# Attention scores in PSUM: three buffers of two banks, visits of up to four units, and VectorE's clamps in pairs

## The chip, the cores and the metric

The kernel runs on one core of a Trainium2 chip. The metric is device time in microseconds, from the first to the last instruction of the core. The kernel before takes 862.6 us (median of three runs, 862.32 to 862.9). An engine runs its own list of instructions in order, and waits on semaphores for the others. TensorE (PE) multiplies matrices and writes to PSUM; PSUM has eight banks of 512 fp32 columns on 128 partitions. ScalarE (ACT) computes the exponentials, VectorE (DVE) copies, clamps and multiplies, GpSimd (POOL) does small scalings, and SyncE (SP) issues transfers.

## The reference, cut to what matters

```python
x = A_x                                    # 1 x 2048 x 640, bf16
g = sigmoid((x * gate_w).sum(-1, keepdims=True))
# A: full attention, 32 heads of 20
scores = einsum("bhqd,bhkd->bhqk", q, k) * 20 ** -0.5
a = (softmax(scores) @ v) @ A_wo
# B: local attention over 8 positions, 2 apart: pos, pos-2, ..., pos-14
logits = where(mask, einsum("bhsd,bhswd->bhsw", q, k[pos - 2 * w]) * 20 ** -0.5, -1e9)
b = (softmax(logits) over w, times v[pos - 2 * w]) @ B_wo
return g * a + (1 - g) * b
```

Branch A is 32 heads x 2048 queries x 2048 keys of exponentials. The kernel calls a piece of 128 keys x 512 queries of one head a *unit*: 32 x 16 x 4 = 2048 units. Each one needs a QK matmul into one PSUM bank, an exponential into SBUF as bf16, and a matmul with V that accumulates in the bank `obank`.

## The kernel before

Most units take their exponential on ScalarE. Some take it on VectorE: the score, already scaled, is clamped and written as a 16-bit integer whose bits read as bf16 are a rough power of two, and three shifted copies with weights (the copies `eD`, and V scaled by GpSimd, `vS`) smooth the error. Four units of one key block and four heads share the same steps.

The whole order of instructions is made on the host by a small scheduler: each task has an assumed duration and an assumed latency to its readers, and side work (projections, branch B, the output projection) is put where TensorE and VectorE are thought to be free.

```python
LAT = {"pe": 0.18, "act": 0.06, "dve": 0.08, "pool": 0.1, "sp": 0.1}   # assumed latency to a reader, by writer
SWITCH = 0.11                                                           # change of TensorE's tiling mode
# ... (cut)
    score = [ps(1536, "score0"), ps(1536, "score1")]      # two buffers of three banks
    obank = ps(512, "obank")
    sbank = ps(512, "side0")
    BANKS = [(sbank, 0), (score[0], 1024), (score[1], 1024)]   # banks for side work; the third of a buffer may be lent
# ... (cut)
    ebuf = [sb([P, 1536], BF16, "ebuf%d" % i) for i in range(NE)]       # NE = 5
# ... (cut)
    def next_tile():
        s = len(tiles)
        x = 1 + s % 2
        # ...
        n = 3 if free else 2       # three units for ScalarE if the third bank is free,
        # ...                      # or two, and one for VectorE ("ride") in the third bank
    def qk(s):
        # ... two or three matmuls, each with 32 rows (one head), into the buffer s % 2
        t = T("pe", 0.215, fn, ..., mode="row")
        if rides[s]:
            run_dve(t.end + LAT["pe"] - RFILL)
            t = T("dve", 0.69, lambda e: e.tensor_scalar(
                uD[d % 2][:, 512 * i:512 * (i + 1)].bitcast(I16), side[x], UOFF, 0.0, op0=ALU.add, op1=ALU.max), ...)
    def exp(s):
        n = len(tiles[s])
        exps[s] = T("act", actc(512 * n), lambda e: e.activation(
            ebuf[s % NE][:, 0:512 * n], score[s % 2][:, 0:512 * n], ACTF.Exp, scale=LN2 / STEP), ...)
# ... (cut)
    def filler(limit):     # matmuls whose result nobody reads, where TensorE would be empty
        # ...
# ... the main loop, per visit s: choose units, QK, exp, attention times V for earlier visits, then side work:
            lim = (exps[s - 1].end if s >= 1 else sch.avail["act"]) + SLACK[max(0, len(us) - 2)]   # SLACK = (0.3, 0.68)
            spend(lim)
```

A *visit* is one such step: QK matmuls for the units of one turn, each unit in a bank of its own. The matmuls of a visit use separate row quarters of the array and run beside one another.

Of the kernel before, what the change touches and what calls it, by code (L numbers as in the profile page):

```python
# [14 lines left out]
P = 128  # L15
# [39 lines left out]
LAT = {"pe": 0.18, "act": 0.06, "dve": 0.08, "pool": 0.1, "sp": 0.1}  # L55
# [20 lines left out]
class _Sched:  # L76
# [49 lines left out]
    def task(self, stream, dur, fn, reads=(), writes=(), dma=False, accum=(), mode="full", nd=1, iss=0.75):  # L126
# [27 lines left out]
        for d in t.deps:  # L154
            d.mark = True
            start = max(start, d.end + LAT[d.stream])
# [104 lines left out]
def _build(ctx, nc, A_x, A_wqkv, A_wo, B_wqkv, B_wo, gate_w, out):  # L261
# [9 lines left out]
    score = [ps(1536, "score0"), ps(1536, "score1")]  # L271
    obank = ps(512, "obank")
    sbank = ps(512, "side0")
    BANKS = [(sbank, 0), (score[0], 1024), (score[1], 1024)]
    NB = len(BANKS)
    side = [t_[:, o_:o_ + 512] for t_, o_ in BANKS]
    sap = lambda b, off, dims: _ap(BANKS[b][0], BANKS[b][1] + off, dims)


    NE = 5  # L280
# [14 lines left out]
    ebuf = [sb([P, 1536], BF16, "ebuf%d" % i) for i in range(NE)]  # L295
# [32 lines left out]
    repB = [sb([P, 2 * TOK], BF16, "repB%d" % i) for i in range(2)]  # L328
# [133 lines left out]
    xheld = [None]  # L462
# [327 lines left out]
    def gen_b(u):  # L790
# [55 lines left out]


# [17 lines left out]
        def taps(w4):  # L865
            T("sp", 2.0 + 0.75 * 4, lambda e: [e.dma_start(repB[w4 % 2][32 * i:32 * i + 32, :], eB[32 * w4:32 * w4 + 32, :])
                                               for i in range(4)], reads=["eB"], writes=[("repB", w4 % 2)], dma=True, nd=4)

        taps(0)
        taps(1)  # L870
        for w4 in range(4):
            for hh in range(2):
                w = 4 * hh + w4
                yield ("dve", DVE_AHEAD, sch.ready(("repB", w4 % 2)))
                vs = vB[:, :, PADB - DIL * w:PADB - DIL * w + TOK]
                rr = _ap(repB[w4 % 2], hh * TOK, [[0, CN], [1, TOK]])
                TB(dvc(CN * TOK, 2), lambda e, w=w, vs=vs, rr=rr: e.tensor_tensor(prodB(w), vs, rr, ALU.mult),  # L877
                  reads=["vB", ("repB", w4 % 2)], writes=[("prod", w)])
            if w4 < 2:
                taps(w4 + 2)  # L880
# [72 lines left out]
    def tail():  # L953
# [14 lines left out]
        b3 = score[1]  # L968
        mm(("score", 1), [fold_mms(b3[:, blk * P:(blk + 1) * P], blk, q, 512, D, False)[0] for blk in range(4)], False)
# [3 lines left out]
        for blk in range(2):  # L973
            mm(("score", 0), fold_mms(score[0][:, blk * 512:(blk + 1) * 512], blk, q, 0, 512, False), False)
        T("dve", dvc(512), lambda e: e.tensor_tensor(
            _ap(stage, 3 * 1024 + 512, [[D, 4], [1, P]]), _ap(b3, 0, [[P, 4], [1, P]]),
            stage[:, 2048:3072].bitcast(FP32).rearrange("p (b c) -> p b c", c=P), ALU.add),
          reads=[("score", 1), ("pre", 2)], writes=["tout_r"])
# [4 lines left out]
        for blk in range(2):  # L983
            T("dve", dvc(512), lambda e, blk=blk: e.tensor_tensor(
                tcol(blk, 0, 512), score[0][:, blk * 512:(blk + 1) * 512], pre(blk), ALU.add),
              reads=[("score", 0), ("pre", blk)], writes=[("tout", blk)])
# [50 lines left out]
    DVE_AHEAD = 0.56  # L1037
    DAHEAD = 0.5

    def step(ent, limit, force):  # L1040
# [14 lines left out]
        elif req[0] == "bank":  # L1055
            best = None
            for b in range(NB):
                if not bank_used[b] and b != xheld[0] and (best is None or max(bank_free[b], now) < max(bank_free[best], now)):
                    best = b
            if best is None or sum(bank_used) == NB - 1 or (not force and bank_free[best] > now):  # L1060
# [15 lines left out]
    BOOST = 4.1  # L1076
    XBOOST = 4.0
    XPRIO = 2.5
    XLATE = 6.3
    XT0 = 144.0  # L1080
    XT1 = 860.0

    def xprio():
        return XPRIO if bdone[0] >= (sch.avail["pe"] - XT0) / (XT1 - XT0) * BALL else XLATE

# [31 lines left out]
    def turn(tcc, c0, c1, s_):  # L1117
        xt, xo = XOFF[tcc]

        def fn(e):  # L1120
            ins = None
            for c in range(c0, c1):
                for blk in range(4):
                    o = score[s_][:, (c - c0) * 512 + blk * P:(c - c0) * 512 + (blk + 1) * P]
# [5 lines left out]
          writes=[("score", s_)] + ([("side", 1)] if c1 - c0 == 3 else []))  # L1130
# [6 lines left out]
    def x_out(tcc):  # L1137
        cols = slice(tcc * 512, (tcc + 1) * 512)
        T("act", actc(1536), lambda e: e.activation(  # L1139
            xT[:, 0:3, cols], _ap(score[0], 0, [[512, 3], [1, 512]]), ACTF.Copy), reads=[("score", 0), ("side", 1)], writes=[("xT", tcc, 0)])  # L1140
# [527 lines left out]
```

## Time and profile before

| | |
|---|---|
| time, median of three | 862.6 us |
| span of the profiled run | 860.4 us |
| visits | 732 |
| exps of 1024 / 1536 columns | 458 / 273 (and one of 512) |
| units clamped by VectorE | 312, each 512 wide |
| first exp starts / last exp ends | 20.7 / 848.5 us |
| busy in 0 to 20 us: PE / DVE / ACT | 16.6 / 13.4 / 10.6 us |
| busy in 840 to 860.4 us: PE / DVE / ACT | 15.3 / 6.1 / 9.2 us |
| TensorE's granted clock | 0.998 |

The profile is of one execution. Its first part gives each engine's busy time, its share of the span and its instructions; its second part cuts the span into 40 slices with a digit for the tenths of busy time. A group of instructions is one row: line, engine, operation, output and input, how often; then its busy time and the mean length of one; then the time the engine was idle just before them and what ended it. "L1432 ACT ... ebuf<-score" are the exponentials, "L1409 PE ... score<-qT,kT" the QK matmuls, "L1422 DVE ... uD<-score" the clamps, "L728 DVE ... eD<-uD" the shifted copies, "L1477 PE ... obank" attention times V, "L1498 PE" the filler and "L489 PE" side work. "PEld" is the loading of weights, at which TensorE's waits show. The waits are rows of: who waited, for whom, microseconds in total, times, the longest. "issue" is time in which nothing was waited for that the profile shows. A timeline row has start, length, what, and in brackets the idle time ahead of it.

### The profile page before, as it was taken

Reading aid. Unit: us, or ns where it says so; the run is one execution under the profiler, and the core shown is the slowest. Engines: PE = TensorE matmul, PEld = TensorE weight load, DVE = VectorE, ACT = ScalarE, POOL = GpSimd, SP = SyncE. Lnnn points to the kernel's source line nnn. Section 1 sums busy time; section 2 is a strip of 40 time slices with the busy share of each in tenths; the row PEclk is TensorE's granted clock in tenths of the full one; section 3 lists DMA queues with packets and bytes.
Section 4 is the critical chain, followed back from the end, with each engine's and each line's share of the span. In section 5 each row is a group of like instructions: output and inputs, shape, how many; then the busy total and the mean of one; then the engine's idle time right before and its main releaser. Section 6 shows DMA issues by size and latency. Waiting matters only on the chain.

```text
span 860.4 us, 30961 instructions
## 1 busy us (share of the span) xinstructions
PE 837.2 (97%) x13299; PEld 310.4 (36%) x13302; DVE 692.4 (80%) x1178; ACT 820.2 (95%) x766; POOL 220.4 (26%) x333
## 2 busy tenths in 40 slices
PE   8999999999999999999999999999999999999997
PEld 4333333343333433333333333333333333333323
DVE  6567787898888889887988879789798878989763
ACT  5999999999999999999999999999999999999994
POOL 5032042721322222221111223222142223123310
PEclk9999999999999999999999999999999999999999
DMA  9112231001010100011010000110010001100000
GB/s 300 33 30 54 45 73 32 16 13 30 25 28 20 38 11 21 5 44 39 18 33 17 6 19 21 32 47 8 20 28 20 6 17 33 46 6 21 14 6 32
DMA packets 40892, 28.16 MB, mean 33 GB/s; under 512 B 23733, under 2 KB 39557, under 8 KB 40757
## 3 DMA queue, kind: packets, MB, share of 16 engines
q1 hardware_dynamic: 40756, 26.20, 11.7%
q8 instruction: 105, 1.72, 0.8%
q14 instruction: 31, 0.25, 0.1%
HBM read 11.94 MB, written 2.62 MB: 17 GB/s over the span
## 4 chain that ended last, share of the span: by engine, by line
PE 77%; ACT 15%; DVE 4%; issue 3%; POOL 1%; DMA 1%; DVEq 0%; ACTq 0%
PE score L1409 23%; PE side L489 19%; PE obank L1477 18%; ACT ebuf L1432 14%; PE score L489 6%; PE obank L1498 4%; PE score L1498 3%; PE side L1498 1%; PE score L615 1%; PE side L814 1%; DMA oTd<-in_A_x_dram 1%; DVE uD L1422 0%; DVE oTt L689 0%; PE score L1125 0%; ACT xT L1139 0%
## 5 line engine op out<-in xcount | busy, mean ns | idle before, releaser
L1432 ACT ACTIVATE ebuf<-score 128x1024 bf16<-128x1024 f32 (+1 forms) x732 | 804.5, 1197 | 19.9 <-PE score L1409 16.0
L1409 PE MATMUL score<-qT,kT 32*128 32x512 bf16 x2048 | 292.1, 384 | 8.7 <-ACT ebuf L1432 6.3
L1422 DVE TENSOR_SCALAR uD<-score 128x512 int16<-128x512 f32 x312 | 208.5, 684 | 41.8 <-PE score L1409 39.3
L720 POOL TENSOR_SCALAR vS<-vA 128x84 bf16<-128x84 bf16 x234 | 140.7, 604 | 230.7 <-PE obank L1477 186.4
L728 DVE TENSOR_SCALAR eD<-uD 128x2048 int16<-128x2048 int16 x234 | 160.2, 709 | 10.3 <-PE obank L1477 9.9
L1409 PEld LDWEIGHTS score<-qT,kT 32*128 32x128 bf16 x2048 | 72.1, 91 | 260.9 <-issue 131.5
L1477 PE MATMUL obank<-ebuf,vA 128*21 128x512 bf16 x1736 | 160.8, 384 | 2.2 <-DVE oTt L689 0.8
L489 PE MATMUL side<-xT,kvw 128*32 128x256 bf16 (+2 forms) x2530 | 102.5, 279 | 0.9 <-DVE dst L593 0.6
L695 POOL TENSOR_TENSOR rcp<-rcp,gA 128x16 f32<-128x16 f32 x31 | 12.3, 397 | 345.3 <-DVE rcp L693 320.8
L1477 PE MATMUL obank<-eD,vS 128*21 128x512 bf16 x936 | 81.0, 379 | 0.0
L489 PEld LDWEIGHTS side<-xT,kvw 128*32 128x32 bf16 (+1 forms) x2530 | 60.5, 96 | 35.0 <-issue 19.8
L1477 PEld LDWEIGHTS obank<-ebuf,vA 128*21 128x21 bf16 x1736 | 39.0, 89 | 81.3 <-issue 63.6
L1498 PE MATMUL obank<-xT,zero 128*32 128x512 bf16 x664 | 56.0, 383 | 0.0
L1498 PE MATMUL score<-xT,ident 128*32 128x512 bf16 x628 | 53.0, 381 | 0.1
L800 DVE TENSOR_TENSOR stage<-qkvB 128x1280 bf16<-128x1280 bf16 x64 | 53.0, 855 | 0.1
L877 DVE TENSOR_TENSOR stage<-qkvB,repB 128x1280 bf16<-128x1280 bf16 x64 | 52.1, 838 | 0.0
L489 PE MATMUL side<-stage,ident 128*32 128x512 bf16 (+1 forms) x768 | 48.7, 346 | 0.0
L784 DVE CAST qkvB<-side 128x512 bf16<-128x512 f32 (+1 forms) x72 | 41.7, 589 | 6.7 <-PE side L489 6.1
L700 POOL TENSOR_TENSOR oN<-oTt,rcp 128x512 bf16<-128x512 f32 x31 | 34.8, 1122 | 2.4
L689 DVE STREAM_TRANSPOSE oTt<-obank 128x512 f32<-128x512 f32 x32 | 22.8, 712 | 14.5 <-PE obank L1477 14.3
L1477 PE MATMUL obank<-uD,vA 128*21 128x512 bf16 x312 | 30.3, 379 | 0.0
L1477 PEld LDWEIGHTS obank<-eD,vS 128*21 128x21 bf16 x936 | 23.4, 92 | 17.5 <-issue 2.5
(167 smaller groups left out, 639.0 us busy)
## 6 DMA issues: line engine op xcount, KB each, us to landing
repB<-eB SPq DMA_DIRECT2D x128, 32.0 KB
WqP<-in_A_wqkv_dram SPq DMA_DIRECT2D x16, 160.0 KB
stage<-in_B_wqkv_dram SPq DMA_DIRECT2D x1, 2400.0 KB
oTd<-oN SPq DMA_DIRECT2D x108, 20.0 KB
qT<-dst SPq DMA_DIRECT2D x104, 20.0 KB
out_dram<-outsb SPq DMA_DIRECT2D x12, 160.0 KB
kvw<-in_A_wqkv_dram SPq DMA_DIRECT2D x2, 800.0 KB
oTd<-in_A_x_dram SPq DMA_DIRECT2D x2, 640.0 KB
```

The lines of the kernel that those rows point to most:

```text
L489: ins = e.matmul(o[j:k, :], l[:, j:k], r, start=(first and i == 0), stop=(last and i == n - 1), skip_group_check=True)
L700: T(en, c2, lambda e: e.tensor_tensor(oo, ii, ib, ALU.mult), reads=["rcp", "oTt"], writes=["oN0"])
L720: T("pool", 0.7, lambda e, k=k: e.tensor_scalar(vS[:, d % 2, k - 1, :], _ap(vA, (kb * NQ + q) * 4 * DV, [[1, 4 * DV]]), WEIGHTS[k], None, ...
L728: T("dve", 0.11 + 0.1334 * n, lambda e, k=k, sl=sl: e.tensor_scalar(eD[:, sl % NS, 0:512 * n].bitcast(I16), uD[d % 2][:, 0:512 * n].bitcas ...
L784: t = TB(dvc(n * TOK), lambda e, o=o, i=i: e.tensor_copy(o, i), reads=[("side", b)], writes=[key])
L800: TB(dvc(CN * TOK, 2), lambda e, w=w, ks=ks: e.tensor_tensor(prodB(w), qB[:, :, :], ks, ALU.mult), reads=["qB", "kB"], writes=[("prod", w) ...
L877: TB(dvc(CN * TOK, 2), lambda e, w=w, vs=vs, rr=rr: e.tensor_tensor(prodB(w), vs, rr, ALU.mult), reads=["vB", ("repB", w4 % 2)], writes=[( ...
L1409: ins = e.matmul(o, kT[32 * j:32 * j + 32, q, kb * P:(kb + 1) * P], qT[g % NQT][32 * j:32 * j + 32, :], start=True, stop=True)
L1422: t = T("dve", 0.69, lambda e: e.tensor_scalar(uD[d % 2][:, 512 * i:512 * (i + 1)].bitcast(I16), side[x], UOFF, 0.0, op0=ALU.add, op1=ALU. ...
L1432: exps[s] = T("act", actc(512 * n), lambda e: e.activation(ebuf[s % NE][:, 0:512 * n], score[s % 2][:, 0:512 * n], ACTF.Exp, scale=LN2 / S ...
L1477: ins = e.matmul(obank[32 * j:32 * j + DV, :], v, src, start=(kb == 0), stop=(last and k >= len(lst) - 4), skip_group_check=True)
L1498: ins = e.matmul(o[32 * j:32 * j + 32, :], w[:, 32 * j:32 * j + 32] if best else w[:, :], xT[:, 0, 0:512], start=bool(best), stop=bool(bes ...
```

## The change

The six banks of the scores become three buffers of two banks. A visit takes the buffers that are free: one of them with two units for ScalarE; or two of them, with four units for ScalarE (two exps of 1024), or two for ScalarE and two for VectorE; or one and a single bank beside it. VectorE's units are clamped in pairs with one instruction 1024 wide where two banks side by side are free. Exps are all 1024 wide, and their SBUF buffers go from five of 1536 to seven of 1024. A side group may take the single side bank or a bank of a score buffer; at most two banks serve side work at a time, and then only of one score buffer. The scheduler's assumed latencies change, now by writer and reader, and with them many constants. Branch B's repeated weights get a third buffer, and their transfers are issued earlier. It is meant to let ScalarE's next work always stand ready and to save VectorE instructions.

```diff
-LAT = {"pe": 0.18, "act": 0.06, "dve": 0.08, "pool": 0.1, "sp": 0.1}
+LAT = {"pe": 0.22, "act": 0.18, "dve": 0.13, "pool": 0.15, "sp": 0.1}
+LATS = {("pe", "act"): 0.28, ("pe", "pool"): 0.29, ("act", "dve"): 0.24, ("dve", "dve"): 0.05, ("dve", "pool"): 0.08,
+        ("pool", "pool"): 0.05, ("act", "act"): 0.02}
...
-            start = max(start, d.end + LAT[d.stream])
+            start = max(start, d.end + LATS.get((d.stream, stream), LAT[d.stream]))
...
-    score = [ps(1536, "score0"), ps(1536, "score1")]
+    scores = ps(3072, "scores")
...
-    BANKS = [(sbank, 0), (score[0], 1024), (score[1], 1024)]
+    NBUF = 3
+    BANKS = [(sbank, 0)] + [(scores, 512 * i) for i in range(2 * NBUF)]
...
-    NE = 5
+    NE = 7
...
-    ebuf = [sb([P, 1536], BF16, "ebuf%d" % i) for i in range(NE)]
+    ebuf = [sb([P, 1024], BF16, "ebuf%d" % i) for i in range(NE)]
...
+    NREP = 3
+    repB = [sb([P, 2 * TOK], BF16, "repB%d" % i) for i in range(NREP)]
...
+    SIDEMAX = 2
...
+    def next_visit():
+        ...
+        free = sorted([i for i in range(NBUF) if i not in ln], key=when)
+        free = free[:1] + [i for i in free[1:] if when(i) <= now + XTOL]
+        ...
+        us = take(2)
+        if us:
+            plan.append((free[0], us))
+            rest = [j for j in range(4) if all(uu % 4 != j for uu in us)]
+            if len(free) > 1:
+                got = wanted(rest, 2, now)
+                if got:
+                    ride = (*got, bk(free[1]))
+                else:
+                    us = take(2)
+                    if us:
+                        plan.append((free[1], us))
...
-            t = T("dve", 0.69, lambda e: e.tensor_scalar(
-                uD[d % 2][:, 512 * i:512 * (i + 1)].bitcast(I16), side[x], UOFF, 0.0, op0=ALU.add, op1=ALU.max),
+            t = T("dve", 0.1 + 0.52 * n, lambda e: e.tensor_scalar(
+                uD[d % 2][:, 512 * i0:512 * (i0 + n)].bitcast(I16), sap(bs[0], 0, [[1, 512 * n]]), UOFF, 0.0, op0=ALU.add, op1=ALU.max),
...
-            lim = (exps[s - 1].end if s >= 1 else sch.avail["act"]) + SLACK[max(0, len(us) - 2)]
+            s += len(plan)
+            lim = (exps[s - 2].end if s >= 2 else sch.avail["act"]) + SLACK        # SLACK = 0.35
...
-        while pvq and len(units) < 12 and pvq[0] // 64 == pvg and tile_of[pvq[0]][0] <= s - 2:
+        while pvq and len(units) < 12 and pvq[0] // 64 == pvg and tile_of[pvq[0]][0] <= s - 2 and (
+                force or exps[tile_of[pvq[0]][0]].end + LAT["act"] <= sch.avail["pe"] + PVTOL):
```

## The prediction

> **What bounds the kernel now.** I read the busy times first, then the groups of instructions by shape, then what each engine waited for, then ScalarE's timeline.
>
> ```profile
> PE 837.2 (97%) x13299; PEld 310.4 (36%) x13302; DVE 692.4 (80%) x1178; ACT 820.2 (95%) x766; POOL 220.4 (26%) x333
> ...
> ACT  5999999999999999999999999999999999999994
> ```
>
> Two engines look full. TensorE's 97% holds work that nobody needs: the filler matmuls of line 1498 (664 + 628 + 340 = 1632, in groups of four).
>
> ```profile
> L1432 ACT ACTIVATE ebuf<-score 128x1024 bf16<-128x1024 f32 x458 | 442.4, 1035 | 12.6 <-PE score L1409 9.9 <-ACT ebuf L1432 0.6
> L1432 ACT ACTIVATE ebuf<-score 128x1536 bf16<-128x1536 f32 x273 | 382.7, 1470 | 7.2 <-PE score L1409 6.2
> ...
> L1422 DVE TENSOR_SCALAR uD<-score 128x512 int16<-128x512 f32 x312 | 208.5, 684 | 41.8 <-PE score L1409 39.3 <-ACT g L679 0.4
> ...
> L1498 PE MATMUL obank<-xT,zero 128*32 128x512 bf16 x664 | 56.0, 383 | 0.0
> L1498 PE MATMUL score<-xT,ident 128*32 128x512 bf16 x628 | 53.0, 381 | 0.1
> ```
>
> ScalarE's exponentials are not filler, and nothing else does them except VectorE's 312 units. So ScalarE is the bound; each microsecond saved must come out of its exps or of the gaps between them.
>
> ```profile
> ACT ebuf L1432 <- PE score L1409: 16.0, 41, 1.0
> ...
> PEld score L1409 <- issue: 131.5, 385, 0.5
> PEld score L1409 <- ACT ebuf L1432: 76.1, 193, 1.0
> ...
> PEld score L1409 <- DVE uD L1422: 22.1, 53, 0.7
> ```
>
> The waits show only 16 us of ScalarE waiting for scores. That is the visible part. The timeline gives the rest:
>
> ```profile
> 150.64 1.94 ACT L1432 ACTIVATE ebuf<-score 128x1024 bf16<-128x1024 f32 x2 [0.25 <-PE score L1409]
> ...
> 512.35 2.80 ACT L1432 ACTIVATE ebuf<-score 128x1536 bf16<-128x1536 f32 x2
> ```
>
> Two narrow exps take 1.94 us although one takes 1.02, so the second starts about 0.92 after the first: neighbours overlap. Two wide ones take 2.80 (one 1.47), a step of 1.33. The start times of the whole trace say the same: the shortest step is 0.904 us after a 1024-wide exp and 1.330 after a 1536-wide one, the mean step 0.964 and 1.39. The account of ScalarE is then:
> - first exp 20.7 us, last one ends at 848.5: a window of 827.8;
> - exps without any gap: 458 x 0.904 + 273 x 1.330 + 0.6 (one 512-wide) = 777.7;
> - other ScalarE work inside (8 eB, 8 tB, 4 g: 5.0 + 3.6 + 0.9, less 20 overlaps of 0.11) = 7.3;
> - slack: 827.8 - 777.7 - 7.3 = 42.8 us, or 58 ns for each of 732 visits. It is spread evenly: each 40 us of trace holds 1 to 3.5 us of it.
>
> Lead-in (20.7) and tail (860.4 - 848.5 = 11.9) have nothing to do with this slack.
>
> **What the Trainium skill says.** ScalarE: Activation LUTs, section What ACT_TABLE_LOAD costs, gives an ACTIVATE with immediate scale 186 ns + 0.833 ns per element, and an overlap of about 93 ns back to back. This would make the step 0.946 us at 1024 and 1.373 at 1536; the trace has 0.904 and 1.330, the same slope ((1330 - 904) / 512 = 0.832 ns) and a smaller fixed part. I use the trace. VectorE: DVE Perf Modes, section Why PSUM operands drop a tier, says that an fp32 read from PSUM has only the 1x mode; the trace agrees: 684 ns for 512 columns, and 1225 ns for the 1024-wide cast of line 1141, is 1.06 ns per column. TensorEngine Tiling (Array Packing), section Key Properties, says that changing the tiling mode drains TensorE. The trace agrees in kind: four-row QK matmuls stand between four-column work, and TensorE's load side sits empty 0.42 to 0.49 us before most of them, and 0.23 after.
>
> **The change part by part.** I took the counts from the instruction lists of the two built programs.
>
> *ScalarE.* 273 exps of 1536, 458 of 1024 and one of 512 become 860 of 1024. Without gaps 860 x 0.904 = 777.4 us, against 777.7. 16 units more go to VectorE (312 to 328), worth 16 x 0.45 = 7 us, and the narrower exps give exactly that back. So the exps themselves save 0.3 us. The whole case hangs on the 42.8 us of slack.
>
> *VectorE.* 312 clamps of 512 become 140 of 1024 and 48 of 512. By 1225 and 684 ns: 140 x 1.225 + 48 x 0.684 = 204 us against 213; the shifted copies eD go from 234 to 246, +12 x 0.71 = 8.5 us. Net about 0. It stays at 80% and is no bound.
>
> *GpSimd.* Twelve more vS copies of 0.60 us at 26% busy: nothing on the path.
>
> *TensorE.* QK matmuls stay 2048. From the scheduler's list of visits: 732 visits before; after 713, of which 147 fill two buffers with four units for ScalarE, 140 give two units to each engine, 48 two and one, 378 two alone. The idle intervals and a QK visit itself displace about 0.43 us (0.64 us from the group in front to the group behind, where column groups follow each other at 0.215). So 19 x 0.43 = -8.2 us. Attention-times-V matmuls rise from 2984 to 3032, 12 groups x 0.215 = +2.6. Filler falls from 1632 to 1452 matmuls, 45 groups x 0.215 = -9.7. Sum -15.3 us. The scheduler puts a filler where TensorE would otherwise stand empty, so less filler with the same work says that it packed the same work into less time. This gives about 862.6 - 15 = 847, independent of ScalarE's account.
>
> *Buffers.* A visit must find its buffer free. Before, with two buffers, ScalarE always has exactly one exp to run (0.904 or 1.33) while TensorE turns round. After, counting exps between the one that frees the buffer and the visit's own: still one in 669 of 713 visits, two or more in about 40. The third buffer is lent to VectorE and to projections, and so rarely deepens the queue. What does change is that the second exp of a four-unit visit, 147 of them, can't wait at all.
>
> *Turn-round.* In the trace an exp that waited started 0.50 us after its visit's first QK matmul (the quartiles of 82 late ones are 0.49 and 0.50), and TensorE starts some 0.05 to 0.11 after the exp that frees it: 0.55 to 0.61 in all. The scheduler before assumes 0.06 + 0.215 + 0.18 = 0.455, so it stuffs side work in front of QK that doesn't fit. After it assumes 0.18 + 0.215 + 0.28 = 0.675: it now leaves too much room rather than too little. This I expect to remove most of the visible waits and a third of the hidden ones.
>
> *Sum.* Visible waits 16.6 us to about 7; hidden 26.2 to about 21: slack 42.8 to 28, -14.8. Exps -0.3. Lead-in and tail 0 (same instructions, other banks). 862.6 - 15 = 847.5; I say 848. How far the slack falls is where I chose; the rest is arithmetic.
>
> **The rivals.**
> - *The cushion is what counts, not the assumed latency.* One exp of cushion stays in 94% of visits, and cushions of 1.33 us become 0.904. For it: nothing structural deepens. Against it: in the trace the mean excess after a wide exp (55 to 68 ns) is no smaller than after a narrow one (56 to 61), so the cushion's length isn't what limits. It would give 713 x 58 ns = 41 us slack, 861 us.
> - *The paired clamp starves ScalarE.* A bank pair is held for 1.2 us where one bank was held for 0.68, and the other VectorE work that empties side banks queues behind it. TensorE waited 22 us for clamps before, in 53 cases. If each of 140 pairs cost 0.15 us more on ScalarE's path: +21 us, 868 at best with nothing else lost. Against: two narrow clamps of 0.684 already run back to back today, and ScalarE has its own buffer meanwhile.
> - *Fixed work can't keep pace.* With one side bank and borrowed pairs, at most two groups at once, the projections and the local attention could end late; the tail (11.9 us) would grow by some 5 to 20 us while ScalarE ends early. For it: TensorE is at 97%. Against: filler is still 1452 matmuls, so room is left until the end.
> - *Nearly all slack goes.* With 15 us left the time would be 835. That is the floor I can imagine.
>
> **Range and chances.** 836 (slack 16) to 862 (no gain) should hold it eight times in ten. Over 2% faster means below 845.3, that is slack below about 26 us: 0.38. Over 2% slower needs a new wait of 17 us on top of everything: 0.05. The rest, 0.57.
>
> **What would show it.** Right: 860 exps with a busy time near 800 us, ScalarE's wait for scores well under 16 us, the last exp ending near 834, lead-in near 21 and tail near 12, and TensorE still near 97%. Wrong: the clamp as the longest releaser of QK, a mean step of exps still at 0.96, a tail above 15 us, or a first exp later than 21.

## The result and the profile after

The changed kernel takes **876.4 us** (median of four runs, 873.98 to 879.32) against 862.5 for the kernel before in the same comparison: a ratio of **1.0162, 95% interval 1.013 to 1.0193**. It is slower by 13.9 us, and outside the range of 836 to 862.

The page of the profile after, parts 1 and 2 (busy times; the tenths of ScalarE and the granted clock in 40 slices of 21.9 us):

```profile
PE 838.3 (96%) x13167; PEld 307.6 (35%) x13170; DVE 695.8 (80%) x1066; ACT 820.3 (94%) x894; POOL 241.8 (28%) x345
...
ACT  5997999999999999999999999999999999999990
...
PEclk9997999999999999999999999999999999999999
```

The three busy times of PE, DVE and ACT are within 4 us of before, so they don't show the loss. The slices do: ScalarE has a 7 in the fourth slice, where TensorE's clock has a 7 as well, and a 0 in the last, where before had a 4. One loss near the beginning, one at the end.

The groups of instructions, exps and filler first, then VectorE's clamps by shape:

```profile
L1469 ACT ACTIVATE ebuf<-scores 128x1024 bf16<-128x1024 f32 x860 | 805.0, 1054 | 23.8 <-PE scores L1444 19.8
...
L1535 PE MATMUL obank<-xT,zero 128*32 128x512 bf16 x636 | 56.2, 384 | 0.0
L1535 PE MATMUL scores<-xT,ident 128*32 128x512 bf16 x680 | 53.3, 380 | 1.0 <-DVE uD L1459 1.0
...
L1459 DVE TENSOR_SCALAR uD<-scores 128x1024 int16<-128x1024 f32 x140 | 170.1, 1215 | 28.8 <-PE scores L1444 28.0
...
L1459 DVE TENSOR_SCALAR uD<-scores 128x512 int16<-128x512 f32 x48 | 32.7, 681 | 19.6 <-PE scores L1444 19.5
```

The exps are there as counted, 805 us busy. A pair is clamped in 1.215 us. Before had 340 filler matmuls in the side bank; here 1452 - 636 - 680 = 136 are left. The scheduler gives filler the side bank first when it is free, so that bank is seldom free now, a hint to what follows.

TensorE's weight loads for QK and for attention times V, with the idle time ahead of them; first the kernel before, then after. Below them two of ScalarE's waits after (who waited for whom, us in total, times, the longest):

```profile
L1409 PEld LDWEIGHTS score<-qT,kT 32*128 32x128 bf16 x2048 | 72.1, 91 | 260.9 <-issue 131.5 <-ACT ebuf L1432 76.1 <-DVE uD L1422 22.1
...
L1477 PEld LDWEIGHTS obank<-ebuf,vA 128*21 128x21 bf16 x1736 | 39.0, 89 | 81.3 <-issue 63.6 <-POOL vS L720 8.5 <-DVE uD L1422 1.4
```

```profile
L1444 PEld LDWEIGHTS scores<-qT,kT 32*128 32x128 bf16 x2048 | 70.7, 91 | 265.1 <-ACT ebuf L1469 166.2 <-issue 54.7 <-DVE uD L1459 35.3
...
L1514 PEld LDWEIGHTS obank<-ebuf,vA 128*21 128x21 bf16 x1720 | 42.6, 88 | 109.1 <-issue 92.4 <-POOL vS L728 8.2 <-POOL kvw L754 1.7
```

```profile
ACT ebuf L1469 <- PE scores L1444: 19.8, 39, 2.4
ACT stage L991 <- PE scores L971: 15.8, 1, 15.8
```

Ahead of QK the idle time as a whole hardly changes (260.9 to 265.1 us); what ends it does: the exps for 76 us before and 166 now, "issue" for 131.5 and 54.7. Ahead of attention times V it grows by 28 us. ScalarE's wait for scores did not fall, 16.0 to 19.8. The last row is one wait of 15.8 us at the end; before it was 6.3.

The account of ScalarE, made as in the prediction (the one exp of 512 is put at 0.48 us here and not at 0.6; tail is the span less the end of the last exp):

| | before | after | difference |
|---|---|---|---|
| first exp | 20.7 | 21.4 | +0.7 |
| exps without gaps | 777.6 | 777.4 | -0.2 |
| other ScalarE work | 7.3 | 7.5 | +0.2 |
| slack | 42.9 | 46.5 | +3.6 |
| tail | 11.9 | 21.3 | **+9.4** |
| span | 860.4 | 874.2 | +13.8 |
| slack of it in 0 to 200 us | 12.4 | 20.4 | +8.0 |
| slack of it in 200 to 840 us | 29.4 | 25.7 | -3.7 |
| units on ScalarE by 160 us | 288 | 272 | -16 |
| units on both engines in 160 to 800 us | 1614 | 1614 | 0 |

(The rest of the slack, 1.0 and 0.4 us, lies after 840 us.) So in the long middle both kernels do the same number of units. The change loses 16 units (about 7 us) before 160 us, doesn't get them back, and then pays 9 us more after the last exp. The windows show both ends. Columns are the busy times of PE, PEld, DVE, ACT and POOL, TensorE's clock, the DMA share and GB/s; first the kernel before, then after:

```profile
20.00:160.00 140.00, 136.80 (x1952) 46.74 (x1952) 100.71 (x188) 134.19 (x130) 37.23 (x46) 1.00 0.20 47
160.00:300.00 140.00, 137.35 (x2311) 53.84 (x2309) 121.34 (x204) 135.99 (x128) 38.70 (x59) 1.00 0.10 24
...
840.00:860.40 20.40, 15.25 (x323) 6.79 (x322) 6.08 (x11) 9.16 (x10) 0.00 (x0) 0.93 0.10 34
```

```profile
20.00:160.00 140.00, 133.93 (x1833) 43.96 (x1833) 95.34 (x175) 128.49 (x140) 28.37 (x41) 0.96 0.16 39
160.00:300.00 140.00, 132.11 (x2013) 46.79 (x2013) 117.61 (x170) 135.55 (x148) 53.50 (x65) 1.00 0.12 30
...
840.00:874.20 34.20, 27.09 (x535) 11.56 (x532) 15.90 (x25) 13.90 (x16) 0.00 (x0) 1.00 0.08 27
```

VectorE does 5.4 + 3.7 = 9.1 us less work before 300 us, and 9.8 us more after 840. What that work at the end is, the timeline of the changed kernel says:

```profile
849.05 1.55 DVE L886 TENSOR_TENSOR stage<-qkvB,repB 128x1280 bf16<-128x1280 bf16 x2
...
853.80 3.64 PE L497 MATMUL scores<-stage,ident 128*32 128x512 bf16 x64
...
858.36 0.42 DVE L901 SCALAR_TENSOR_TENSOR oB<-side,rB 128x256 bf16<-128x256 f32 x1 [0.18 <-PE side L497]
858.84 0.46 PE L497 MATMUL scores<-woBp,oB 128*32 128x128 bf16 x20 [0.53 <-DVE oB L901]
...
868.67 0.60 ACT L991 ACTIVATE stage<-side 128x512 bf16<-128x512 f32 x1 [15.79 <-PE scores L971]
```

It is branch B, the local attention. Its last tap products (V times weight) are at 849, its last sums over the taps at 853.8, after the last exp (852.9), and its last result `oB` at 858.4. Only then can the rest of the output projection run. The kernel before had its last `oB` 42 us earlier, while the exps still ran:

```profile
816.65 0.41 DVE L892 SCALAR_TENSOR_TENSOR oB<-side,rB 128x256 bf16<-128x256 f32 x1
...
854.82 1.09 ACT L981 ACTIVATE stage<-score 128x512 bf16<-128x512 f32 x2 [6.34 <-PE score L962]
```

### The profile page after: what moved, and what is told of

It reads as the page before. It is cut to its first block, busy times and chain, and to the rows that moved or that the text cites. A ratio compares the mean times of both kernels' runs of the same rounds, so it can differ in the third digit from the quotient of the medians.

```text
span 874.2 us, 30670 instructions
## 1 busy us (share of the span) xinstructions
PE 838.3 (96%) x13167; PEld 307.6 (35%) x13170; DVE 695.8 (80%) x1066; ACT 820.3 (94%) x894; POOL 241.8 (28%) x345
## 4 chain that ended last, share of the span: by engine, by line
PE 60%; DVE 17%; ACT 17%; issue 4%; POOL 1%; DMA 0%; DVEq 0%; SPq 0%; ACTq 0%
PE scores L1444 18%; ACT ebuf L1469 16%; PE obank L1514 15%; PE side L497 13%; PE scores L497 6%; DVE uD L1459 5%; PE scores L1535 3%; DVE eD L736 3%; PE obank L1535 2%; DVE stage L808 2%; DVE qkvB L792 2%; DVE stage L886 1%; DVE oTt L697 1%; PE side L822 1%; DVE oN L710 1%
## 5 line engine op out<-in xcount | busy, mean ns | idle before, releaser
L1469 ACT ACTIVATE ebuf<-scores 128x1024 bf16<-128x1024 f32 x860 | 805.0, 1054 | 23.8 <-PE scores L1444 19.8
L1444 PE MATMUL scores<-qT,kT 32*128 32x512 bf16 x2048 | 290.4, 386 | 14.8 <-ACT ebuf L1469 4.6
L1459 DVE TENSOR_SCALAR uD<-scores 128x1024 int16<-128x1024 f32 (+1 forms) x188 | 202.8, 1079 | 48.4 <-PE scores L1444 47.5
L728 POOL TENSOR_SCALAR vS<-vA 128x84 bf16<-128x84 bf16 x246 | 160.7, 657 | 179.2 <-PE obank L1514 136.9
L1514 PE MATMUL obank<-ebuf,vA 128*21 128x512 bf16 x1720 | 170.8, 388 | 6.5 <-DVE oTt L697 1.9
L1444 PEld LDWEIGHTS scores<-qT,kT 32*128 32x128 bf16 x2048 | 70.7, 91 | 265.1 <-ACT ebuf L1469 166.2
L497 PE MATMUL side<-xT,kvw 128*32 128x256 bf16 (+1 forms) x2540 | 104.7, 279 | 3.3 <-DVE qkvB L792 1.9
L497 PEld LDWEIGHTS side<-xT,kvw 128*32 128x32 bf16 x2540 | 61.9, 96 | 34.3 <-issue 11.9
L1535 PE MATMUL scores<-xT,ident 128*32 128x512 bf16 x680 | 53.3, 380 | 1.0 <-DVE uD L1459 1.0
L710 DVE STREAM_TRANSPOSE oN<-oN 128x512 bf16<-128x512 bf16 x32 | 22.5, 704 | 12.0 <-POOL oN L708 10.7
```

Source lines behind the costliest of these rows:

```text
L497: ins = e.matmul(o[j:k, :], l[:, j:k], r, start=(first and i == 0), stop=(last and i == n - 1), skip_group_check=True)
L728: T("pool", 0.7, lambda e, k=k: e.tensor_scalar(vS[:, d % 2, k - 1, :], _ap(vA, (kb * NQ + q) * 4 * DV, [[1, 4 * DV]]), WEIGHTS[k], None, ...
L1444: ins = e.matmul(side[b], kT[32 * j:32 * j + 32, q, kb * P:(kb + 1) * P], qT[g % NQT][32 * j:32 * j + 32, :], start=True, stop=True)
L1459: t = T("dve", 0.1 + 0.52 * n, lambda e: e.tensor_scalar(uD[d % 2][:, 512 * i0:512 * (i0 + n)].bitcast(I16), sap(bs[0], 0, [[1, 512 * n]]) ...
L1469: exps[s] = T("act", actc(512 * n), lambda e: e.activation(ebuf[s % NE][:, 0:512 * n], scores[:, 1024 * i:1024 * i + 512 * n], ACTF.Exp, s ...
L1514: ins = e.matmul(obank[32 * j:32 * j + DV, :], v, src, start=(kb == 0), stop=(last and k >= len(lst) - 4), skip_group_check=True)
```

## The experiments

Three questions: what the loss at the beginning is; why branch B is late; and which part of the change does what in the middle. All ratios are against the kernel before (862.8 to 863.3 beside these runs).

### The early loss: e1 and e2

Timeline of the changed kernel around 70 us:

```profile
68.44 1.14 SPq L643 DMA_DIRECT2D qT<-qbnd  x2
70.77 0.15 PEld L1444 LDWEIGHTS scores<-qT,kT 32*128 32x128 bf16 x6 [2.84 <-issue]
70.80 0.61 PE L1444 MATMUL scores<-qT,kT 32*128 32x512 bf16 x6 [2.54 <-DMA qT<-qbnd]
...
71.30 1.94 ACT L1469 ACTIVATE ebuf<-scores 128x1024 bf16<-128x1024 f32 x2 [2.44 <-PE scores L1444]
...
72.75 1.03 PE L1444 MATMUL scores<-qT,kT 32*128 32x512 bf16 x3
...
74.52 0.61 PE L1444 MATMUL scores<-qT,kT 32*128 32x512 bf16 x2
...
78.50 0.61 PE L1514 MATMUL obank<-ebuf,vA 128*21 128x512 bf16 x4
...
82.76 0.39 PE L1444 MATMUL scores<-qT,kT 32*128 32x512 bf16 x2
```

A visit takes units for VectorE from the *next* group of heads, whose Q depends on a bound that is still on its way: the transfer is issued at 68.44 and TensorE, which runs in order, stands 2.54 us for it. ScalarE idles 2.44. From 72.1 to 82.3 us a visit of two takes 0.61 where it takes 0.39 at 82.76; the granted clock (the column behind the busy times) is half there:

```profile
70.80:72.09 1.29, 1.29 (x22) 0.55 (x26) 0.85 (x1) 0.79 (x1) 0.00 (x0) 1.00 0.00 0
72.09:82.33 10.24, 10.24 (x78) 2.08 (x74) 4.55 (x8) 6.27 (x8) 0.00 (x0) 0.50 0.01 2
```

Two things could cost the time: the wait, or the slower TensorE after it. e1 takes the wait away, e2 keeps it and keeps TensorE busy through it.

e1, the next group's units are taken only once their Q has landed:

```diff
-                if done.get(("q", g)) and t_end >= now + DTIME:
+                if done.get(("q", g)) and t_end >= now + DTIME and sch.ready(*qkeys[g]) <= now:
```

> The changed kernel, but VectorE may start on a unit of the next head group only when that group's Q and its bound have landed in SBUF. Theory A (an early stall plus a late branch B): the wait for the bound's transfer near 70 us goes, TensorE's clock stays full, ScalarE's slack between 40 and 80 us falls from 8 us to under 2, at 100 us ScalarE has done 165 to 172 units instead of 152. The tail of 21 us stays, because it has another cause, so the time falls by 5 to 8 us to 868 to 871. Theory B (the paired clamps starve the others): the early stall is a detail that is made up for later; no change within 2 us.

Measured: 875.2 us, ratio 1.0134 (1.0119 to 1.0149). The loss at the beginning is gone: 164 units done by 100 us (after: 152, before: 168), slack up to 200 us 11.8. But the order of everything behind it is remade: the slack from 200 to 840 is 31.8 (after: 25.7), 5.6 us of it between 680 and 720 us, VectorE takes 324 units instead of 328, and the tail stays at 19.8. So most of what came in was given back.

e2, filler matmuls (zero weights, nothing is added to `obank`) where TensorE would wait more than 0.6 us for Q:

```diff
+        while sch.ready(*rd) > sch.avail["pe"] + 0.6:
+            # four matmuls, zero x xT, accumulating into obank
+            T("pe", 0.215, warm_fn, reads=["zero", ("xT", 0, 0)], accum=["obank"], mode="col")
```

> The changed kernel in its own order, with filler matmuls placed in front of a QK visit that would wait over 0.6 us for a transfer. The stall stays, TensorE isn't empty in it. Theory A with the clock as the larger part of the early loss: granted clock 0.998 or more, matmuls between 71 and 82 us back to 0.39 us, slack between 40 and 80 us down to 3 to 4 us, time 870 to 873, and the spread between runs (874 to 879) shrinks below 1 us. If the clock doesn't matter: same time and spread.

Measured: 872.1 us (871.65 to 872.79), ratio 1.0099 (1.0082 to 1.0116). Timeline of this run:

```profile
67.73 2.98 PE L1456 MATMUL obank<-xT,zero 128*32 128x512 bf16 x52
...
70.64 0.61 PE L1444 MATMUL scores<-qT,kT 32*128 32x512 bf16 x6
...
71.15 1.94 ACT L1478 ACTIVATE ebuf<-scores 128x1024 bf16<-128x1024 f32 x2 [2.65 <-PE scores L1444]
...
72.37 0.60 PE L1444 MATMUL scores<-qT,kT 32*128 32x512 bf16 x3
```

ScalarE waits as long as before (2.65 us), yet the visit of three that took 1.03 takes 0.60, no slice has a clock below 9, and 162 units are done by 100 us; the slack up to 200 us is 17.1. The time falls by 4.3 us (the intervals of the two ratios don't overlap) and the spread between runs from 5.3 to 1.1 us. So of the early loss some 4 us were TensorE's clock after the stall, not the wait itself. The four runs of the changed kernel have mean clocks of 0.993, 0.992, 0.988 and 0.987 at 874.0, 876.1, 876.7 and 879.3 us, so a slower clock goes with a longer time in them too.

The stall alone doesn't decide how much clock is lost. TensorE stands for 2.5 to 3.0 us at this place in six traces (the changed kernel, e3, e6, e7, e11, e12), and the spell at half the clock that begins there lasts 10.2, 10.2, 3.4, 13.7, 0 and 13.7 us. TensorE: Matmul & The Clock Gate, section What's actually happening, of the Trainium skill says that the clock falls to half after an idle window of about 3.4 us, and that the window runs free. The traces agree on the length and the free running: the spells at half the clock, away from both ends of the program, last whole steps of 3.41 us and begin on one grid within a trace. But the window need not be empty: in the 3.41 us before the fall at 72.09 us TensorE was busy for 38%. In e11 the stall lay across two such windows, busy for 66 and 47%, and no fall came.

### Parts of the change one at a time: e3, e4, e5

e3, the pair of units clamped in two instructions of 512 instead of one of 1024:

```diff
-            t = T("dve", 0.1 + 0.52 * n, lambda e: e.tensor_scalar(uD[...][:, 512 * i0:512 * (i0 + n)], ...),
+            t = T("dve", 0.1 + 0.52 * n, lambda e: [e.tensor_scalar(uD[...][:, 512 * (i0 + k):512 * (i0 + k + 1)], ...)
+                for k in range(n)][-1],
```

> The changed kernel in its own order, with each clamp of 1024 columns as two of 512, both banks released after the second. Theory A: VectorE is busy 140 x 0.06 to 0.14 = 8 to 20 us longer, and since it isn't the bound in steady state the time moves by under 4 us. Theory B (the time that VectorE holds the bank pair is what costs): it holds the pair 0.06 to 0.14 us longer each time, and the time grows by 8 to 20 us.

Measured: 879.2 us, ratio 1.0185 (1.0163 to 1.0208), VectorE busy for 703.6 us against 695.8. The paired clamp saves 7.8 us of VectorE and by the medians 2.9 us of time (the intervals of the two ratios overlap, so the second figure is uncertain). It is not the cause of the loss.

e4, the changed kernel with the assumed latencies of before; e5, the kernel before with those of after. Nothing else is changed:

```diff
 # e4 (e5 the other way round, in the kernel before)
-LAT = {"pe": 0.22, "act": 0.18, "dve": 0.13, "pool": 0.15, "sp": 0.1}
-LATS = {("pe", "act"): 0.28, ("pe", "pool"): 0.29, ("act", "dve"): 0.24, ...}
+LAT = {"pe": 0.18, "act": 0.06, "dve": 0.08, "pool": 0.1, "sp": 0.1}
+LATS = {}
```

> The changed kernel with the assumed latencies of the kernel before (0.18, 0.06, 0.08, 0.1, 0.1; one per writer). Theory A: the structure and not the latencies costs, so the time stays within 5 us of the changed kernel, 871 to 881. Theory C (the longer assumed latencies make the scheduler leave room that isn't used): back to 860 to 866, with more filler.

> The kernel before with the assumed latencies of the changed kernel, by writer and reader, and nothing else. The reverse (old latencies in the changed kernel) cost 14 us. Theory C (the new latencies are better by themselves, the new structure costs): this one gains, 850 to 860. Theory D (the constants of each kernel were chosen for its own latencies, and a remade schedule is worse until they are chosen again): 865 to 872, with branch B late and a tail over 15 us.

| time (slack, tail) | old latencies | new latencies |
|---|---|---|
| buffers of before | 862.5 (42.9, 11.9) | e5: 870.5 (36.1, 19.6), ratio 1.0089 (1.0074 to 1.0104) |
| buffers of after | e4: 890.4 (62.0, 20.3), ratio 1.0316 (1.03 to 1.0331) | 876.4 (46.5, 21.3) |

The new latencies cut the slack by 6.8 us in one structure and 15.5 in the other. But little of it is where they were meant to act: between 200 and 840 us it is 29.4 and 27.5 in the upper row, 28.8 and 25.7 in the lower, and most of the rest lies before 200 us, where e4 has two stalls of TensorE of its own, 3.7 and 3.1 us. ScalarE's wait for scores doesn't fall in e5 (16.9 us against 16.0), nor does QK's wait for "issue" (128.0 against 131.5); in e4 that wait is 58.7, so what lowers it is the new structure. In the old structure alone the new latencies make the kernel 8 us slower: VectorE gets 296 units instead of 312, so the exps are 784.6 us instead of 777.6, and the tail goes to 19.6, although branch B may still borrow banks there. What is left of the change (three buffers, their visits, their constants) has more slack at either latency: 46.5 - 36.1 = 10.4 us with the new ones, 62.0 - 42.9 = 19.1 with the old. With the new ones all of it comes before 200 us (20.4 against 8.0); later the three buffers have less (25.7 against 27.5).

### Moving branch B: e6 and e7

VectorE takes units only while branch B is on a line from `BT0` (230 us) to `BT1` that the scheduler's constants set. e6 draws that line steeper:

```diff
-    BT1 = 872.0
+    BT1 = 830.0
```

> The changed kernel with BT1 = 830 in place of 872: VectorE starts new groups of units only while branch B keeps a faster pace. Theory A: branch B ends about 30 us earlier and the tail falls from 21 to 11 or 12 us. What it costs shows whether the tail was an accident of order or the price of VectorE's time: an accident gives 864 to 868; if VectorE has no time to spare, there are about 12 more exps on ScalarE (11 us) and the time stays at 873 to 879.

Measured: 878.7 us, ratio 1.0184 (1.0169 to 1.0199). The page and the end of the timeline of this run:

```profile
PE 836.8 (96%) x13127; PEld 308.9 (35%) x13130; DVE 670.5 (77%) x1032; ACT 830.8 (95%) x906; POOL 222.0 (25%) x327
```

```profile
863.77 1.02 ACT L1469 ACTIVATE ebuf<-scores 128x1024 bf16<-128x1024 f32 x1 [0.26 <-PE scores L1444]
870.55 0.60 ACT L991 ACTIVATE stage<-side 128x512 bf16<-128x512 f32 x1 [5.75 <-PE scores L971]
```

The last `oB` ends at 825.7 and the tail is 11.2, shorter than before the change, with the rule of lending left as it is. So the long tail of the changed kernel is branch B's lateness, and an earlier branch B takes it away. But VectorE got 304 units instead of 328, so there are 872 exps: 788.3 us without gaps, +10.9, and the gain is gone. Compared with the kernel before at the same tail, exps cost 10.7 us more. Of these about 3.6 are the eight units fewer on VectorE (8 x 0.45); the other 7.1 are the width: a unit costs ScalarE 0.904 / 2 = 0.452 us in an exp of 1024 and 1.330 / 3 = 0.443 in one of 1536, and 273 x 3 = 819 units lost their wide exps (819 x 0.0087 = 7.1). VectorE is busy for only 670.5 us here, so it was not out of time; by the edit it is the line that held its share back.

e7 lets every kind of side work borrow a bank of the score buffers at any time; before, branch B could do so only when it was late:

```diff
-    XPRIO = 1.0
-    XLATE = 1.0
+    XPRIO = 8.0
+    XLATE = 8.0
```

> The changed kernel with XPRIO and XLATE at 8, so that branch B and the other side work may take banks of the score buffers too, as they could take the third bank of a buffer before. Lending one bank takes a buffer of two from the scores. If the single side bank is what holds branch B back, B ends earlier and the time falls below 870. If the lent buffer is missed more (theory A's reading of one side bank less: it can't be had back), ScalarE's slack grows by 10 us or more, and the time rises to 880 to 890.

Measured: 891.9 us, ratio 1.0323 (1.03 to 1.0346). Waits of this run:

```profile
PEld scores L1444 <- issue: 70.2, 218, 2.9
ACT ebuf L1469 <- PE scores L1444: 50.4, 88, 2.7
```

ScalarE's visible waits go from 19.8 to 50.4 us and the slack to 84.8 (profiled in the slowest of the four runs, at a mean clock of 0.973, so some of this is TensorE's clock). A bank lent is half of one of three buffers, and the other half can then take a unit for VectorE or a second side group, but no exp; before, a lent bank was the third of a buffer whose other two banks went on taking two units. The tail is 12.0. So lending at all times costs far more than it brings; the old rule itself (only urgent work, and branch B when late) was not tried in the changed kernel.

### Leaving out work of the last B unit: e11 and e12

e11 leaves out the eight tap products of branch B's last unit, e12 the projections of that unit (it takes q, k and v of the unit before). Both change what is computed for 256 positions; they are here for the times alone.

```diff
 # e11, in the loop over the taps
+                if u == 2 * QCN - 1:
+                    continue
 # e12, at the head of the projections of unit u
+        if u == 2 * QCN - 1:
+            done[("bqk", u)] = done[("bproj", u)] = True
+            return
```

> The changed kernel without the eight tap products of branch B's last unit (its output is left wrong for the last 256 positions): 8 x 0.82 = 6.6 us less work on VectorE, the same number of grants of the single side bank. Theory A (the end of branch B is late because its groups pass one after another through one side bank): the tail stays near 21 us (19 to 22) and the time within 3 us of the changed kernel's 876. Theory B (VectorE comes too late to branch B): the tail falls by 5 to 9 us, to 12 to 16, and the time to 867 to 871.

> The changed kernel without branch B's projections for its last unit (it uses the q, k and v of the unit before): eight groups less through the side banks, each of which holds a bank for about 2.5 to 3 us, so 20 to 24 us of bank time, about 5 us of VectorE and 15 us of TensorE's side work (32 matmuls groups of 256 columns). Theory A (one side bank): branch B's last unit ends earlier by about 20 us, the tail falls to about 12 us and the time to 864 to 868. Theory B (VectorE's time): the gain is that of 5 us of VectorE's work, the tail falls by no more than in the run without tap products.

Measured: e11 873.6 us, ratio 1.0123 (1.0106 to 1.014), tail 20.0; e12 875.9, ratio 1.0151 (1.0125 to 1.0176), tail 18.3. In both the last `oB` still comes 4 to 5 us *after* the last exp. With less work the last unit is not done sooner: from one unit's `oB` to the next it is 60 us in the changed kernel, 61 in e11, 66 in e12. e11 fits theory A (the side bank), e12 contradicts what A said of it, and the gain that theory B expected did not come in either. The line counts the work that is left out as work not done, which may be why VectorE's share went down in e12 (322 units). So these two runs don't tell the theories apart.

### The rule of lending, in the kernel before: e13, e14, e15

The cleaner test takes only the rule into the kernel before. e13: branch B (urgency 6.0) may never borrow a third bank (nor may the few kinds of work at 3 and 4). e14: nor may anything but the most urgent work, so that the sums ahead of the output projection (2.2 to 2.4) and the projections of Q and K (1.1, 1.2) may not either. e15: the output projection goes ahead of branch B (5.0 against 6.0), as in the changed kernel.

```diff
 # e13
-    XLATE = 6.3
+    XLATE = 2.5
 # e14
-    XPRIO = 2.5
-    XLATE = 6.3
+    XPRIO = 1.0
+    XLATE = 1.0
 # e15
-    PF = 6.6
+    PF = 5.0
```

> The kernel before with one rule of the changed kernel: branch B may never take a third bank of a score buffer for its groups, not even when it is late (work of urgency 2.5 or better still may). Everything else, the two buffers, the exps of 1536 and the assumed latencies, stays. Theory A (one side bank is what makes branch B late, and branch B makes the tail): the last oB comes some 30 us later than 817, the tail grows from 12 to 17 to 20 us, the last exp ends where it did (846 to 850), and the time is 868 to 872. Theory C (the tail comes from the pace that the scheduler's target line gives branch B, and from VectorE's share of the units): nothing changes, 863 within 2 us, with the tail at 11 to 13.

> The kernel before with both lending figures of the changed kernel: only work of urgency 1.0 or better may take a third bank, so the sums ahead of the output projection may not either. Theory A: tail 17 to 20 us, last oB near 850, and besides more thirds for ScalarE (fewer and wider exps); time 873 to 880, that is, like the changed kernel, although the buffers are the old ones. Theory C: 863 within 2 us.

> The kernel before with the changed kernel's order of urgency for the output projection: 5.0 in place of 6.6, so ahead of branch B (6.0) and no longer behind it. Theory A: the lent banks are still there, so little changes, 861 to 865. Theory D (it is the output projection going ahead of branch B that makes the latter late): the last oB near 840, tail 16 to 20, time 868 to 872.

Measured: e13 869.7 us, ratio 1.0077 (1.0062 to 1.0093); e14 873.3, ratio 1.0116 (1.0101 to 1.0131); e15 864.8, ratio 1.0029 (1.0018 to 1.004). Timeline of e13:

```profile
831.65 1.55 DVE L877 TENSOR_TENSOR stage<-qkvB,repB 128x1280 bf16<-128x1280 bf16 x2
...
834.57 0.40 PE L489 MATMUL side<-woBp,oB 128*32 128x512 bf16 x4 [0.77 <-DMA oTd<-oN]
...
844.10 0.73 PE L489 MATMUL score<-woA_d,oTd 128*32 128x512 bf16 x8
844.75 0.61 PE L489 MATMUL side<-stage,ident 128*32 128x512 bf16 x8
...
851.87 1.01 DVE L892 SCALAR_TENSOR_TENSOR oB<-score,rB 128x512 bf16<-128x512 f32 x2
...
861.81 0.60 ACT L981 ACTIVATE stage<-score 128x512 bf16<-128x512 f32 x1 [13.91 <-PE score L962]
```

In e13 everything else is as it was: 312 units on VectorE, the last exp ends at 847.9 (before 848.5), slack 41.9. The tap products are done at 833, but the banks are with the sums ahead of the output projection (`woBp`, `woA_d`) until 844, and branch B's sums (`stage,ident`) begin only then. Its last `oB` ends at 852.9 instead of 817.1, and the tail is 20.1 instead of 11.9. So the rule alone costs 8.2 us of tail and 6.9 us of time, as theory A had it; theory C's "nothing changes" falls. e14 no longer computes the reference's result (off by a relative 0.027), and what in its order spoils it is not known, so nothing is built on it; its tail is 21.0, and VectorE takes only 296 units. e15 is a small thing, tail 11.4: with lending allowed, the order of urgency costs 2 us.

In the structure of the changed kernel the same order of events shows in e1, where the tap products are early enough:

```profile
835.39 1.54 DVE L886 TENSOR_TENSOR stage<-qkvB,repB 128x1280 bf16<-128x1280 bf16 x2
...
844.26 0.93 PE L497 MATMUL side<-woA_d,oTd 128*32 128x512 bf16 x12
846.10 0.60 PE L497 MATMUL side<-stage,ident 128*32 128x512 bf16 x8
...
855.70 0.41 DVE L901 SCALAR_TENSOR_TENSOR oB<-scores,rB 128x256 bf16<-128x256 f32 x1
```

They are done at 836.9, 15 us before the last exp, but the one side bank is with the output projection, and the sums begin at 846.1. In the changed kernel itself that wait is only 3.2 us (850.6 to 853.8), since its tap products are late already.

Over all 17 kernels the tail is 10.6 to 12.0 us in the five where the last `oB` ends before the last exp (before, e6, e7, e8, e15), and 18.3 to 21.3 in the twelve where it ends 4 to 6 us after it. Both fit one reading: the program ends some 11 us after the last exp or 14 to 16 us after the last `oB`, whichever is later. The rule isn't the only way to the long tail: e5 (19.6, new latencies) and the run e10 below (20.3, one width of exps) have it in the kernel before with the old rule of lending, and e4 keeps it (20.3) in the changed kernel with the old latencies.

### Constants chosen again, and the width alone: e8, e9, e10

The kernel before was tuned for its latencies, and the changed one for its own. e8 is the kernel before with the new latencies and 23 scheduling constants chosen again; e9 the changed kernel with the condition of e1 and its constants chosen again.

```diff
 # e8 (cut to some of those that touch branch B and the lending)
+LAT, LATS as in the changed kernel
-    XLATE = 6.3
+    XLATE = 6.583
-    DLOW = 6.7
+    DLOW = 7.983
-    PB = 6.0
-    PP = 6.5
-    PF = 6.6
+    PB = 6.205
+    PP = 6.634
+    PF = 6.826
 # e9 (cut likewise)
+    e1's condition
-    XPRIO = 1.0
-    XLATE = 1.0
+    XPRIO = 2.021
+    XLATE = 3.98
-    PB = 6.0
-    PF = 5.0
+    PB = 4.998
+    PF = 4.128
```

> The kernel before with the assumed latencies of the changed kernel and its constants (paces, priorities, thresholds) chosen again for them by trying 600 sets on the host's own schedule. Theory A: the calibrated latencies are the good half of the change and the structure the bad half; this one has less slack on ScalarE than before (under 38 us), a tail of 10 to 12 us, and takes 856 to 860, less than both kernels. Theory D in its strong form (any constants fit only the old latencies): 863 or more.

> The changed kernel with the check on landed transfers and its constants chosen again in the same way and from as many sets. If the three buffers are as good as two and only their constants were poor: within 3 us of the run with two buffers, 856 to 860. Theory A: narrow exps cost ScalarE 7 us for the same units, which comes back as a longer window or a longer tail: 863 to 868.

Measured: e8 **856.7 us**, ratio 0.9928 (0.9916 to 0.9941), faster than both kernels; e9 865.4, ratio 1.0031 (1.0023 to 1.004). Waits and the end of e8:

```profile
PEld score L1411 <- issue: 115.5, 344, 0.5
...
ACT ebuf L1434 <- PE score L1411: 14.6, 34, 0.9
```

```profile
849.33 0.60 ACT L983 ACTIVATE stage<-side 128x512 bf16<-128x512 f32 x1 [5.04 <-PE side L964]
```

Both are near in the window from first to last exp, 822.6 and 821.6 us (slack 34.0 and 38.0; exps 781.1 and 775.6). Of the 7.3 us between their spans the tail makes 8.5 (10.6 against 19.1), lead-in and window the rest. So at their best here the two structures differ by the end of branch B, not by how ScalarE is fed.

e10 asks whether one width of exps is worth anything by itself: the kernel before, where a visit may never take a third unit for ScalarE.

```diff
-                if ride:
-                    break
+                break
```

> The kernel before, never three units in one exp: all exps 1024 wide, two buffers, the third bank for VectorE's unit or side work alone. What one width costs: 868 exps of 1024 in place of 458 and 273 would be 785 us in place of 777.6 for the same 312 units on VectorE. Theory A: 7 us more at least, and more slack since there are about 140 more visits (each at 58 ns: 8 us): 876 to 882. If the width doesn't matter (the exps overlap well enough): 862 to 866.

Measured: 886.7 us, ratio 1.0279 (1.0265 to 1.0293): 874 exps of 1024, 790.1 without gaps (+12.5), slack 46.1 (+3.2), tail 20.3 (+8.4). Uniform exps bring nothing by themselves. At the same old latencies the three buffers (e4, 890.4 us) are no better than two buffers with exps of one width.

## Why the prediction was wrong

In the terms of the prediction's own sum, two steps failed: the slack was to fall from 42.8 to 28 us and is 46.5 (18.5 us too much), and the tail was to stay at 11.9 us and is 21.3 (9.4). Lead-in adds 0.7; the exps were right.

- **ScalarE is the bound; the middle is exps plus slack**: right for 160 to 800 us, where both kernels do the same 1614 units. But a bound on the middle is not a bound on the end, and the prediction treated it as one.
- **Exps 777.4 against 777.7**: right (777.4). What stood beside it, "16 units more go to VectorE (312 to 328), worth 16 x 0.45 = 7 us, and the narrower exps give exactly that back", was booked as zero. It is a zero on ScalarE only. e6 shows the other side of the entry: with branch B as early as before, VectorE takes 304 units, and exps cost 10.7 us more.
- **VectorE net about 0**: right (692.4 to 695.8 us), clamps 1.215 us for an estimated 1.225. The sum hid that 9 us of it moved from before 300 us to after 840.
- **TensorE, "less filler with the same work says that it packed the same work into less time"**: failed. The reading gave 847. The time in which the profile has no matmul running did not shrink, it grew from 860.4 - 837.2 = 23.2 to 874.2 - 838.3 = 35.9 us, and the weight loads for attention times V stood idle 28 us longer. Filler fell without a gain: the side bank, where it goes first, was seldom free for it (340 to 136).
- **Buffers, cushion of one exp in 94% of visits**: the prediction said that nothing structural deepens, and expected no loss. From 200 us on that holds: at equal new latencies the three buffers have no more slack than two (25.7 against 27.5). Before 200 us they have 12 us more, of which e1, without the early stall, takes away 8.6 (though its remade order has 31.8 later).
- **Turn-round, slack 42.8 to 28**: failed. The new latencies do lower the slack, by 6.8 us in e5, but by only 1.9 between 200 and 840 us, and the visible waits that were to fall from 16.6 to about 7 are 16.9 in e5 and 19.8 in the changed kernel. There the slack is 3.7 us lower than before between 200 and 840, and 8.0 higher before 200. Two other prices were missed: with the new latencies VectorE gets 16 units fewer, and the tail grows by 7.7 us (e5).
- **"Lead-in and tail 0 (same instructions, other banks)"**: failed, +0.7 and +9.4 us. The same instructions came in another order: branch B's last result moved behind the last exp, and the output projection waits for it. e6 moves it back and has a tail of 11.2. What makes it late has more than one sufficient cause in the kernel before: the rule of lending (e13), the latencies (e5), the width of the exps (e10).
- **The rival "Fixed work can't keep pace"** said 5 to 20 us of tail, and came true with 9.4. It was set aside because "filler is still 1452 matmuls, so room is left until the end". Filler in `obank` and in the score buffers shows TensorE's room, not a free bank; the row that counts, filler in the side bank, had fallen from 340 to 136.
- **The early stall** was in no rival. Three of the named signs of being wrong came: a first exp later than 21 us (21.4), a tail above 15 (21.3) and a mean step of exps still at 0.96 (0.960). But a visit that waits for the next head group's Q was not looked for.
- **The paired clamp starves ScalarE**: rightly set aside; the pair is a gain (e3).

What stays open is which part of the change makes branch B late in the changed kernel. Its last tap products end at 850.6 us (before: 803.0), so branch B's slower pace comes first and the wait for the bank on top of it; e11 and e12 could not separate them. That the rule by itself makes 8.2 us is shown in the kernel before alone. Why the three buffers have 19 us more slack with the old latencies (e4) was not taken apart further than the early stalls.

## What to carry to other kernels

When a change takes banks or buffers from background work, follow that work's last result to the end of the program: here the tail was 11 or 20 us, with the last `oB` before or after the last exp. A lower number of fillers or the same busy time isn't proof of better packing; look at where the filler went and in which stretch the work lies. And constants tuned around a structure belong to it: the new latencies cost 8 us beside the old constants (e5), and with constants chosen again the same kernel is 6 us faster than before (e8; what the constants alone would bring was not tried).

## What was unexpected of the hardware

A stretch of 2.5 us without a matmul was followed by 10.2 us at half the clock, in which a visit of two took 0.61 instead of 0.39 us and a visit of three 1.03 instead of 0.60; keeping TensorE busy with matmuls that nobody needs was worth 4.3 us and most of the spread between runs. The same stall cost between nothing (e11, 2.96 us across two windows) and 13.7 us of half clock (e7, e12), so one profile of it says little about the next run.
